# Soft MoE on linear attention: neighbouring loads joined into longer rows, their homes moved, and the last products and output chunks reordered

## The chip, the cores and the metric

The kernel runs on one core of one Trainium2 chip. The core has a matrix engine (PE, with a separate weight-load slot PEld), a vector engine (DVE), an activation engine (ACT), a general engine (POOL), and a queue engine (SP), which here only issues DMA transfers. 16 DMA engines move the bytes between HBM and the core's on-chip memory of 128 partitions. The metric is device time in microseconds, and less is better.

## What is computed

```python
kv = einsum('bhsd,bhse->bhde', k, v)            # 8 batches, 8 heads, 576 tokens, 64 wide
out = einsum('bhsd,bhde->bhse', q, kv)
x = out / sqrt(mean(out**2, -1) + 1e-6) * g_norm  # 4608 tokens x 512
logits = x @ phi                                # 32 slots: 8 experts x 4
d = exp(logits - logits.max(0));  d /= d.sum(0) + 1e-9
slot_input = d.T @ x
for e in range(8):                              # w1[e] 512 x 1024, w2[e] 1024 x 512
    slot_out[e] = relu(slot_input[e] @ w1[e]) @ w2[e]
c = exp(logits - logits.max(1));  c /= c.sum(1) + 1e-9
return c @ slot_out                             # 4608 x 512
```

All numbers are float32. Inputs are some 62 MB, half tokens and half expert weights, and the output is 9.4 MB.

## The kernel before

The host lays every input out so that each of the 128 partitions reads one contiguous piece. `kv` of a batch is 4608 floats (18 KB) per partition, and `q` of two batches together is as much. Each expert has one unit of `w1` and one of `w2`, of 4096 floats (16 KB) per partition. The `w2` units from 2 on are cut by output half: units 2, 3, 4 hold half 0 of experts 2 to 7, and units 5, 6, 7 hold half 1 of the same experts.

On chip one buffer, `arena`, of 160 KB per partition, holds all of it in turn. Tables give each piece its home, in KB: `KV_AT`, `Q_AT` and `W_AT` (line 36 on). `w1` of expert 7 has no home in the arena and goes into the buffer `xall` of the normalised tokens, once these are used up. The order of everything is written out by hand; no scheduler moves instructions.

The stages follow each other:

- Token phase. 36 tiles of 128 tokens (variable `T`, in order) go through products with the batch's `kv` matrix (`products`, line 236), squares, eviction, norm and logits. A batch's `kv` is made in three steps just ahead of the first tile that needs it: batch `b` starts at `first[b]`, and its `kv` tile is read at tiles `first[b]-3` and `first[b]-2`. Per group of 6 tiles an online softmax over tokens adds to the slot sums (`group_*`).
- Expert phase. `expert_h(e)` makes the hidden layer of expert e, `expert_y(e, hf)` adds its half `hf` of the output to `pY`. `combine(k)` makes the weights `c` for a third of the tokens.
- Output. `gather(hf)` copies a half of `pY`, `mix(hf)` makes the matrix `z`, and `output(hf, k, f)` makes one of six chunks of a half: four matmuls into two PSUM tiles `po`, one copy on ACT (line 655), one on DVE (line 657), and one transfer of 768 KB to HBM. PSUM tiles with tag `m` are three, shared by `po`, `ph` and `pz`.

All transfers are issued by SP, in program order. A load that must wait for its home (until PE has read the last of what lay there) holds back all loads behind it. The transfers then queue at the 16 DMA engines, in order of issue. Before the token phase SP issues 13 (lines 107 to 119); four groups more hang on tiles in `loads_behind` (line 122), and the rest of the weights are placed between the steps of the tail and of the expert phase.

`fill` puts matmuls on zeros where PE would idle.

Of the kernel before, what the change touches and what calls it, by code (L numbers as in the profile page):

```python
# [25 lines left out]
CT = 12  # L26
NCH = NT // CT
NX = 14
EARLY = (18, 2, 0)
LATE_FILL = (21, 5, 5, 2, 2)  # L30
TOK = 4608
UNIT = 4096
KB = 256
ARENA = 160 * KB
LATE = 6
KV_AT = (0, 36, 54, 90, 108, 0, 18, 36)
Q_AT = (18, 72, 142, 54)
W_AT = {
# [3 lines left out]
}  # L42
SCRATCH = 1024
EPS_RMS = 1e-6
EPS_SUM = 1e-9


@with_exitstack
def soft_moe_linear_attention(ctx: ExitStack, tc: tile.TileContext, kv_in, q_in, w1_in, w2_in, c_in, out):


    nc = tc.nc
# [11 lines left out]
    def place(at, n):  # L64
        return arena[:, at * KB : at * KB + n]

    def load_kv(b, g=None):
        lo, hi = (0, TOK) if g is None else (2304 * g, 2304 * g + 2304)
        nc.sync.dma_start(place(KV_AT[b], TOK)[:, lo:hi], kv_in[b, :, lo:hi])

    def load_q(g, half=None):
        lo, hi = {None: (0, TOK), 0: (0, 2048), 1: (2048, TOK)}[half]
        nc.sync.dma_start(place(Q_AT[g], TOK)[:, lo:hi], q_in[g, :, lo:hi])

    def kv_main(b, g):
        return place(KV_AT[b], TOK)[:, g * 2304 : g * 2304 + 2048]

    def kv_rest(b, g):
        return place(KV_AT[b], TOK)[:, g * 2304 + 2048 : g * 2304 + 2304]

    def q_main(b):
        return place(Q_AT[b // 2], TOK)[:, b % 2 * 2048 : b % 2 * 2048 + 2048].rearrange("p (r n) -> p r n", r=NPAIR)

    def q_rest(g):
        return place(Q_AT[g], TOK)[:, 4096:].rearrange("p (i r n) -> p i r n", i=2, r=NPAIR)


    def homes(kind, u):
        at = W_AT[kind, u]
        if at is None:  # L90
            return [xflat[:, :UNIT]]
        return [place(a, UNIT // len(at)) for a in at]

    def load_w(kind, u):
        parts = homes(kind, u)
        n = UNIT // len(parts)
        for i, t in enumerate(parts):
            nc.sync.dma_start(t, (w1_in if kind == "w1" else w2_in)[u, :, i * n : i * n + n])

    def w_block(kind, u, i):  # L100
        parts = homes(kind, u)
        n = UNIT // len(parts)
        k, at = divmod(i * 256, n)
        return parts[k][:, at : at + 256]


    load_kv(0, 0)
    nc.sync.dma_start(cst, c_in)
    load_kv(0, 1)
    load_q(0, 0)  # L110
    load_kv(1, 0)
    load_kv(1, 1)
    load_q(0, 1)
    load_kv(2)
    load_q(1, 0)
    load_kv(3)
    load_q(1, 1)
    load_kv(4)
    load_q(2)


    loads_behind = {
        9: lambda: (load_kv(5), load_kv(6), load_q(3), load_kv(7)),
        18: lambda: [load_w(k, e) for e in range(2) for k in ("w1", "w2")],
        27: lambda: [load_w("w1", e) for e in range(2, 5)],
        31: lambda: load_w("w1", 5),
    }

    nc.scalar.preload_act_table_set("natural_log_exp_and_others")
# [15 lines left out]
    for i in range(2):  # L145
        lo = 64 * i
# [20 lines left out]
    class Kv:  # L167
# [10 lines left out]
        def products(self, r):  # L178
            g, w = divmod(r, 2)
            main = kv_main(self.b, g).rearrange("p (r w c n) -> p r w c n", r=2, w=2, c=4)  # L180
            for c in range(4):
                for i in range(2):
                    lo = 64 * i
                    nc.tensor.matmul(  # L184
                        self.pkv[lo : lo + 64, w, g],
                        lhsT=main[:, w, 1, c, lo : lo + 64],
                        rhs=main[:, w, 0, c, lo : lo + 64],
                        start=c == 0 and (g == 0 or self.b == 0),
                        stop=False,
                    )  # L190
# [43 lines left out]
    sqs, mss, parts, r0s, rs_of = {}, {}, {}, {}, {}  # L234
# [201 lines left out]

    fill(EARLY[0])

    for g in range(2):
        kv = Kv(0, "o" if g else "kv", 2 if g else None)  # L440
        kv.products(2 * g)
        kv.products(2 * g + 1)
        kv.borders((g,))
        kv.slots((g,))
        fill(EARLY[1 + g])
    T_at, diag_at, pb_at, d_at, sums_at = {}, {}, {}, {}, {}
    for T in range(NT - 2):
        for b in range(1, B):
# [2 lines left out]
        o = products(T)  # L451
# [64 lines left out]
    group_max(G)  # L516
    for i in todo_sums:
        group_sum(*i)
    load_w("w1", 6)
    load_w("w1", 7)  # L520
    load_w("w2", 2)
    fill(LATE_FILL[0], home=ps.tile([P, 512], F32, tag="m", name="fill"), cols=512)
    group_max_T(G)
    group_max_row(G)
# [86 lines left out]
    def expert_y(e, hf):  # L611
        u, at = w2_unit(e, hf)
        for c in range(8):
            j = c % 4
            nc.tensor.matmul(  # L615
                pY[32 * j : 32 * j + 32, hf, :256],
                lhsT=hTs[e][:, c],
                rhs=w_block("w2", u, at + c),
                start=e == 0 and c < 4,
                stop=e == NE - 1 and c >= 4,  # L620
            )
# [16 lines left out]

    def output(hf, k, f):
        z = zs[hf]  # L640
        at = 6 * ((hf * NCH + k) * 2 + f)
# [16 lines left out]
        nc.sync.dma_start(out[hf, k, :, f], place(at, 4 * CT * NS))  # L658

    def halves(e):  # L660
        expert_y(e, 0)
        expert_y(e, 1)

    expert_h(0)
    load_w("w2", 3)
    expert_h(1)
    halves(0)
    load_w("w2", 4)
    load_w("w2", 5)
    combine(0)  # L670
    expert_h(2)
    halves(1)
    load_w("w2", 6)
    load_w("w2", 7)
    combine(1)
    for e in range(3, NE):
        expert_h(e)
# [3 lines left out]
        expert_y(e, 0)  # L681
    chunks = [(k, f) for k in range(NCH) for f in range(2)]
    gather(0)
    expert_y(2, 1)
    mix(0)
    expert_y(3, 1)
    output(0, *chunks[0])
    output(0, *chunks[1])
    expert_y(4, 1)
    expert_y(5, 1)  # L690
    output(0, *chunks[2])
    output(0, *chunks[3])
# [10 lines left out]
def build_program():  # L703
    import concourse.bacc as bacc

    nc = bacc.Bacc("TRN2", target_bir_lowering=False, num_devices=1, dynamic_dma_scratch_size=SCRATCH)
    shapes = {"kv": (B, P, TOK), "qt": (B // 2, P, TOK), "w1": (NE, P, UNIT), "w2": (NE, P, UNIT), "cs": (P, 129)}
# [48 lines left out]
```

## Time and profile before

| | |
|---|---|
| Runs | 176.03, 177.60, 177.36 us; median 177.36 |
| Profiled execution | 175.97 us, its span 174.2 us |
| Mean granted PE clock | 0.973 |
| Transfers issued by SP | 46: 16 for tokens, 17 for weights, 1 for constants, 12 for output |
| HBM | 61.93 MB read, 9.44 MB written |

The span runs from the first to the last instruction, and the profiled execution's own time has 1.8 us more around it. The transfers by kind, with the line's columns: what is written and read, how many, the size of one, and the median time from issue to landing:

```profile
arena<-in_w_dram SPq DMA_DIRECT2D x14, 2048.0 KB, 20.7
arena<-in_kv_dram SPq DMA_DIRECT2D x6, 2304.0 KB, 30.4
out_dram<-arena SPq DMA_DIRECT2D x12, 768.0 KB, 6.5
```

A time to landing counts everything that the transfer has to queue behind. Window rows give, for a stretch of the span, its length, each engine's busy time with its instructions, the granted PE clock, the busy share of the 16 DMA engines and what they moved. A share slightly above 1 comes from packets whose recorded times overlap a little.

### The profile page before, as it was taken

The page shows a single profiled execution, that of the slowest core. Times are in us where ns is not written, and L with a number is a line of the kernel's source. Part 1 is how long each engine was busy: PE and PEld are TensorE (multiplying, and loading weights), DVE is VectorE, ACT ScalarE, POOL GpSimd, SP SyncE. Part 2 cuts the span into 40 slices and gives each one's busy share as a digit, 9 for nine tenths or more (in the row PEclk, how much of TensorE's full clock was granted, in tenths as well). Part 3 has the DMA queues.
Part 4 walks back from the last instruction along what each step waited for, and adds up shares of the span by engine and source line. Part 5 has one row for each costly group of instructions (what it writes and reads, how often), then busy time and mean ns, then how long its engine had stood idle before and what let it go on. Part 6 is the DMA issues. An engine that isn't in the chain of part 4 may idle for free.

```text
span 174.2 us, 4772 instructions
## 1 busy us (share of the span) xinstructions
PE 148.2 (85%) x2024; PEld 108.9 (63%) x2024; DVE 88.3 (51%) x180; ACT 86.8 (50%) x224; POOL 55.7 (32%) x65
## 2 busy tenths in 40 slices
PE   7577799999989899999999769989999959989500
PEld 5456778889779788888996555456556424445200
DVE  1122156566486565466663778733888114457600
ACT  2036286986957957878779553102234003336400
POOL 6000067656546676266773568000000000000000
PEclk9999999999999999999999999999999999999955
DMA  5999999999999999999999999999999999999994
GB/s 188 416 429 426 439 414 432 420 432 440 414 432 423 421 431 420 420 427 436 429 418 419 433 418 433 429 429 406 440 421 419 425 425 426 386 398 406 419 419 199
DMA packets 6645, 71.68 MB, mean 411 GB/s; under 512 B 736, under 2 KB 864, under 8 KB 2400
## 3 DMA queue, kind: packets, MB, share of 16 engines
q1 hardware_dynamic: 6624, 71.37, 97.5%
q8 instruction: 16, 0.26, 0.6%
q14 instruction: 5, 0.04, 0.1%
HBM read 61.93 MB, written 9.44 MB: 410 GB/s over the span
## 4 chain that ended last, share of the span: by engine, by line
PE 46%; DMA 20%; ACT 11%; DVE 11%; issue 3%; POOL 2%; SPq 1%; POOLq 0%; DVEq 0%
PE o L252 17%; DMA arena<-in_w_dram 11%; DMA arena<-in_kv_dram 9%; PE kvp_kv L184 8%; PE po L647 5%; PE pY L615 4%; PE ph L597 3%; DVE logits L329 3%; PE pS L386 2%; DVE ms L275 2%; ACT arena L655 2%; POOL part L324 2%; ACT bd L219 2%; PE o L243 2%; ACT sq L262 2%
## 5 line engine op out<-in xcount | busy, mean ns | idle before, releaser
L252 PE MATMUL o<-bd,arena 128*128 128x192 f32 x256 | 49.4, 336 | 1.4 <-ACT xall L270 0.6
L252 PEld LDWEIGHTS o<-bd,arena 128*128 128x128 f32 x256 | 40.8, 190 | 4.7 <-ACT xall L270 1.6
L302 POOL TENSOR_TENSOR xall<-xall,r 128x512 f32<-128x512 f32 x34 | 34.8, 1044 | 0.0
L324 POOL TENSOR_TENSOR part<-part,r 128x512 f32<-128x512 f32 x17 | 17.8, 1049 | 51.5 <-DVE r L293 51.5
L329 DVE TENSOR_REDUCE logits<-part 128x64 f32<-128x512 f32 (+1 forms) x19 | 19.3, 1015 | 16.1 <-POOL part L324 16.0
L275 DVE TENSOR_REDUCE ms<-sq 128x16 f32<-128x1024 f32 (+1 forms) x19 | 22.0, 1156 | 6.2 <-ACT sq L262 6.2
L262 ACT ACTIVATE sq<-o 128x512 f32<-128x512 f32 x36 | 21.5, 596 | 6.5 <-PE o L252 5.9
L270 ACT COPY xall<-o 128x512 f32<-128x512 f32 x34 | 20.6, 607 | 0.0
L184 PE MATMUL kvp_kv<-arena 128*64 128x64 f32 x480 | 17.3, 225 | 3.6 <-DMA arena<-in_kv_dram 3.6
L655 ACT COPY arena<-po 128x768 f32<-128x768 f32 x12 | 9.3, 800 | 20.2 <-DMA arena<-in_w_dram 10.3
L184 PEld LDWEIGHTS kvp_kv<-arena 128*64 128x64 f32 x480 | 15.2, 138 | 6.5 <-DMA arena<-in_kv_dram 4.5
L615 PE MATMUL pY<-arena,xall 128*32 128x256 f32 x256 | 15.2, 380 | 2.4 <-DMA arena<-in_w_dram 2.4
L657 DVE COPY arena<-po 128x768 f32<-128x768 f32 x12 | 11.3, 956 | 8.0 <-PE po L647 7.2
L647 PE MATMUL po<-logits,z 32*128 32x384 f32 x96 | 13.7, 526 | 1.6 <-ACT arena L655 1.0
L615 PEld LDWEIGHTS pY<-arena,xall 128*32 128x32 f32 x256 | 8.0, 110 | 9.1 <-issue 3.2
L597 PE MATMUL ph<-arena,sTe 128*32 128x256 f32 x224 | 12.7, 379 | 0.3 <-DVE sTe L544 0.3
L269 ACT COPY part<-o 128x256 f32<-128x256 f32 x34 | 12.6, 371 | 0.0
L386 PE MATMUL pS<-xall,d 128*32 128x129 f32 x288 | 10.7, 276 | 2.1 <-ACT d L374 2.1
L283 ACT ACTIVATE r<-ms,eps 128x16 f32<-128x16 f32 x17 | 5.2, 308 | 12.8 <-DVE ms L275 12.6
L647 PEld LDWEIGHTS po<-logits,z 32*128 32x128 f32 x96 | 6.3, 183 | 8.2 <-ACT arena L655 4.1
L291 DVE SCALAR_TENSOR_TENSOR r<-ms,r 128x16 f32<-128x16 f32 x17 | 3.0, 175 | 15.3 <-ACT r L284 15.3
L597 PEld LDWEIGHTS ph<-arena,sTe 128*32 128x32 f32 x224 | 7.2, 110 | 5.2 <-DVE sTe L544 0.6
(88 smaller groups left out, 143.9 us busy)
## 6 DMA issues: line engine op xcount, KB each, us to landing
arena<-in_w_dram SPq DMA_DIRECT2D x14, 2048.0 KB, 20.7
arena<-in_kv_dram SPq DMA_DIRECT2D x6, 2304.0 KB, 30.4
out_dram<-arena SPq DMA_DIRECT2D x12, 768.0 KB, 6.5
arena<-in_kv_dram SPq DMA_DIRECT2D x4, 1152.0 KB, 10.1
arena<-in_qt_dram SPq DMA_DIRECT2D x2, 2304.0 KB, 32.1
arena<-in_qt_dram SPq DMA_DIRECT2D x2, 1280.0 KB, 23.2
arena<-in_qt_dram SPq DMA_DIRECT2D x2, 1024.0 KB, 16.4
xall<-in_w_dram SPq DMA_DIRECT2D x1, 2048.0 KB, 15.4
```

Source lines behind the costliest of these rows:

```text
L184: nc.tensor.matmul(self.pkv[lo : lo + 64, w, g], lhsT=main[:, w, 1, c, lo : lo + 64], rhs=main[:, w, 0, c, lo : lo + 64], start=c == 0 and ...
L252: nc.tensor.matmul(o[:, r, :192], lhsT=q_main(2 * g + i)[:, r, at : at + P], rhs=bds[i][:, r], start=True, stop=True)
L262: nc.scalar.activation(sqs[s][:, T - starts[s]], o[:, :, 32:160], AF.Square, scale=0.125)
L270: nc.scalar.copy(xts[T % NX][:, :, :128], o[:, :, 32:160])
L275: nc.vector.tensor_reduce(out=mss[s], in_=sqs.pop(s).rearrange("p t j (w d) -> p (t j w) d", w=2), axis=AX.X, op=ALU.add)
L302: nc.gpsimd.tensor_tensor(out=x, in0=x, in1=r[:, i].rearrange("p (j w) -> p j w", w=2).unsqueeze(3).to_broadcast([P, 4, 2, D]), op=ALU.mult,)
L324: engine.tensor_tensor(out=part, in0=part, in1=rs_of[s].unsqueeze(3).to_broadcast([P, STAGES[s], H, NS]), op=ALU.mult)
L329: nc.vector.tensor_reduce(out=L[:, pos(starts[s]) : pos(starts[s]) + STAGES[s]], in_=parts.pop(s).rearrange("p t h n -> p t n h"), axis=AX ...
L386: nc.tensor.matmul(pS[32 * j : 32 * j + 32], lhsT=ds[G][:, i], rhs=x[:, j], start=i == 0, stop=i == GROUPS[G] - 1)
L597: nc.tensor.matmul(ph[32 * j : 32 * j + 32], lhsT=sTe[:, (4 * e + c) * NS : (4 * e + c + 1) * NS], rhs=w_block("w1", e, 4 * c + j), start= ...
L615: nc.tensor.matmul(pY[32 * j : 32 * j + 32, hf, :256], lhsT=hTs[e][:, c], rhs=w_block("w2", u, at + c), start=e == 0 and c < 4, stop=e == ...
L647: nc.tensor.matmul(po[:, u, : CT * NS].rearrange("p (g x) -> p g x", g=2), lhsT=z[lo : lo + 32, f * P : (f + 1) * P], rhs=cT[k][lo : lo + 32],
```

## The change

Six transfers fewer, each larger, over the same bytes:

- `kv` 4 and `q` 2 become one tensor `t2` with rows of 36 KB; `kv` 6, `q` 3 and `kv` 7 become `t3` with rows of 54 KB; `kv` 5 stays alone. `kv` 0 to 3 and `q` 0 and 1 move to one tensor `head`, and are loaded in the same pieces and order as before.
- The weights lie in one flat tensor in the order of use. The first three loads each bring two units in rows of 32 KB: (w1 0, w2 0), (w1 1, w2 1), (w1 2, w1 3). All later units come singly.
- Homes are new, so that the parts of a joined row lie side by side: `kv` 3 goes where `kv` 0 was, `q` 2 behind `kv` 4, and `kv` 6, `q` 3, `kv` 7 over `q` 0, `kv` 1, `kv` 2.
- Loads hang on other tiles: the second pair on tile 21, the third on 26; one half of w2 2 comes ahead of w1 6. The three units of half 1 are all issued behind expert 1's products.
- The output buffers move up by 16 KB.
- At the end `mix(0)` and two chunks of half 0 come before the half 1 products of experts 2 and 3, one chunk more before experts 4 and 5, two more before 6 and 7; the last stands behind `gather(1)` instead of `mix(1)`.
- The first fills are half as many at twice the width.

```diff
-EARLY = (18, 2, 0)
+EARLY = (9, 1, 0)
...
-KV_AT = (0, 36, 54, 90, 108, 0, 18, 36)
-Q_AT = (18, 72, 142, 54)
+KV_AT = (0, 36, 54, 0, 90, 126, 18, 54)
+Q_AT = (18, 72, 108, 36)
...
+W_ROWS = (2, 2, 2, 1, 1, 1, 1, 1, 1, 1, 1, 1, 1)
...
+    def load_row(at, src):
+        nc.sync.dma_start(place(at, src.shape[-1]), src)
...
-    def load_w(kind, u):
-        parts = homes(kind, u)
-        n = UNIT // len(parts)
+    def load_w(*units, part=None):
+        lo = W_ORDER.index(units[0])
+        n = UNIT * len(units)
+        row = w_in[:, lo * UNIT * P : (lo * UNIT * P) + n * P].rearrange("o (p n) -> (o p) n", p=P)
+        parts = homes(*units[0])
+        if len(units) > 1:
+            parts = [place(W_AT[units[0]][0], n)]
...
     loads_behind = {
-        9: lambda: (load_kv(5), load_kv(6), load_q(3), load_kv(7)),
-        18: lambda: [load_w(k, e) for e in range(2) for k in ("w1", "w2")],
-        27: lambda: [load_w("w1", e) for e in range(2, 5)],
-        31: lambda: load_w("w1", 5),
+        9: lambda: load_row(KV_AT[6], t3_in),
+        18: lambda: load_w(("w1", 0), ("w2", 0)),
+        21: lambda: load_w(("w1", 1), ("w2", 1)),
+        26: lambda: load_w(("w1", 2), ("w1", 3)),
+        27: lambda: load_w(("w1", 4)),
+        31: lambda: (load_w(("w1", 5)), load_w(("w2", 2), part=1)),
     }
...
+    load_head(5, 0, TOK)
+    load_head(4, 2048, TOK)
+    load_row(KV_AT[4], t2_in)
+    load_row(KV_AT[5], kv5_in)
...
     halves(0)
-    load_w("w2", 4)
-    load_w("w2", 5)
+    load_w(("w2", 4))
     combine(0)
     expert_h(2)
     halves(1)
-    load_w("w2", 6)
-    load_w("w2", 7)
+    load_w(("w2", 5))
+    load_w(("w2", 6))
+    load_w(("w2", 7))
...
     gather(0)
-    expert_y(2, 1)
     mix(0)
-    expert_y(3, 1)
     output(0, *chunks[0])
     output(0, *chunks[1])
+    expert_y(2, 1)
+    expert_y(3, 1)
+    output(0, *chunks[2])
     expert_y(4, 1)
     expert_y(5, 1)
-    output(0, *chunks[2])
     output(0, *chunks[3])
+    output(0, *chunks[4])
     expert_y(6, 1)
     expert_y(7, 1)
     gather(1)
-    output(0, *chunks[4])
+    output(0, *chunks[5])
     mix(1)
-    output(0, *chunks[5])
```

The change moves instructions at two places. The first is SP's queue from `kv` 3 on, first before, then after (a row: line, operation, what is written and read, partitions x elements of a transfer, and in brackets the semaphores it waits for: DMAHW is another transfer's landing, PE the matrix engine).

```order
L69 DMA arena_64<-in_kv_dram 128x4608 [waits DMAHW1_49]
L73 DMA arena_64<-in_qt_dram 128x2560 [waits DMAHW2_49]
L69 DMA arena_64<-in_kv_dram 128x4608 [waits DMAHW3_49]
L73 DMA arena_64<-in_qt_dram 128x4608 [waits DMAHW4_49]
L69 DMA arena_64<-in_kv_dram 128x4608 [waits DMAHW5_49,PE_49]
L69 DMA arena_64<-in_kv_dram 128x4608 [waits DMAHW6_49,PE_49]
L73 DMA arena_64<-in_qt_dram 128x4608 [waits DMAHW7_49]
L69 DMA arena_64<-in_kv_dram 128x4608 [waits DMAHW0_49]
L98 DMA arena_64<-in_w1_dram 128x4096 [waits DMAHW2_49,DMAHW1_49,PE_49]
L98 DMA arena_64<-in_w2_dram 128x4096
L98 DMA arena_64<-in_w1_dram 128x4096 [waits DMAHW3_49]
L98 DMA arena_64<-in_w2_dram 128x4096 [waits DMAHW4_49]
```

```order
L71 DMA arena_64<-in_head_dram 128x4608 [waits DMAHW2_49,DMAHW1_49,PE_49]
L71 DMA arena_64<-in_head_dram 128x2560
L74 DMA arena_64<-in_t2_dram 128x9216 [waits DMAHW3_49]
L74 DMA arena_64<-in_kv5_dram 128x4608 [waits DMAHW4_49]
L74 DMA arena_64<-in_t3_dram 128x13824 [waits DMAHW6_49,DMAHW7_49,DMAHW5_49,PE_49]
L106 DMA arena_64<-in_w_dram 128x8192 [waits DMAHW2_49,DMAHW3_49,DMAHW0_49,PE_49]
L106 DMA arena_64<-in_w_dram 128x8192 [waits DMAHW4_49,PE_49]
```

Twelve transfers became seven; `kv` 3, the first row of each, now waits for PE too, and of the weights each pair waits for PE by itself.

The second place is PE's queue in the output stage, from the products that end half 0, before and after (pY collects the experts' products, pz is the mix, po an output chunk's PSUM tile: half, third, f, v).

```order
L615 MATMUL pY_1464<-arena_64,xall_65 32x256 x56
L635 MATMUL pz0_1753<-y0_1743,sel_93 128x256
L615 MATMUL pY_1464<-arena_64,xall_65 32x256 x8
L647 MATMUL po0_0_0_0_1765<-logits_104,z0_1755 128x384 x2
L647 MATMUL po0_0_0_1_1769<-logits_104,z0_1755 128x384 x2
L647 MATMUL po0_0_1_0_1774<-logits_104,z0_1755 128x384 x2
L647 MATMUL po0_0_1_1_1778<-logits_104,z0_1755 128x384 x2
L615 MATMUL pY_1464<-arena_64,xall_65 32x256 x16
```

```order
L625 MATMUL pY_1448<-arena_64,xall_65 32x256 x48
L645 MATMUL pz0_1729<-y0_1727,sel_89 128x256
L657 MATMUL po0_0_0_0_1733<-logits_100,z0_1731 128x384 x2
L657 MATMUL po0_0_0_1_1737<-logits_100,z0_1731 128x384 x2
L657 MATMUL po0_0_1_0_1742<-logits_100,z0_1731 128x384 x2
L657 MATMUL po0_0_1_1_1746<-logits_100,z0_1731 128x384 x2
L625 MATMUL pY_1448<-arena_64,xall_65 32x256 x16
```

Before, 8 products of expert 2 for half 1 stood ahead of the mix and 8 of expert 3 behind it; now all 16 stand behind the first two chunks.

More of the change, by code (lines that the diff above doesn't have):

```diff
@@ L35 @@
 LATE = 6
-KV_AT = (0, 36, 54, 90, 108, 0, 18, 36)
-Q_AT = (18, 72, 142, 54)
+KV_AT = (0, 36, 54, 0, 90, 126, 18, 54)
+Q_AT = (18, 72, 108, 36)
 W_AT = {
[3 rows of a table removed]
-}
[3 rows of a table added]
+}
+W_ROWS = (2, 2, 2, 1, 1, 1, 1, 1, 1, 1, 1, 1, 1)
+W_ORDER = [("w1", 0), ("w2", 0), ("w1", 1), ("w2", 1)] + [("w1", e) for e in range(2, NE)] + [("w2", u) for u in range(2, NE)]
 SCRATCH = 1024
@@ L48, in soft_moe_linear_attention @@
 @with_exitstack
-def soft_moe_linear_attention(ctx: ExitStack, tc: tile.TileContext, kv_in, q_in, w1_in, w2_in, c_in, out):
+def soft_moe_linear_attention(ctx: ExitStack, tc: tile.TileContext, head_in, t2_in, kv5_in, t3_in, w_in, c_in, out):
     nc = tc.nc
@@ L65, in place, with load_head @@
         return arena[:, at * KB : at * KB + n]
[L67 to L73, printed above, removed]
+    def load_head(u, lo, hi):
+        at = (KV_AT[0], KV_AT[1], Q_AT[0], KV_AT[2], Q_AT[1], KV_AT[3])[u]
+        nc.sync.dma_start(place(at, TOK)[:, lo:hi], head_in[u, :, lo:hi])
+    def load_row(at, src):
+        nc.sync.dma_start(place(at, src.shape[-1]), src)
     def kv_main(b, g):
@@ L92, in homes @@
         return [place(a, UNIT // len(at)) for a in at]
-    def load_w(kind, u):
-        parts = homes(kind, u)
-        n = UNIT // len(parts)
+    def load_w(*units, part=None):
[5 more added lines that the diff above has]
+            parts = [place(W_AT[units[0]][0], n)]
         for i, t in enumerate(parts):
-            nc.sync.dma_start(t, (w1_in if kind == "w1" else w2_in)[u, :, i * n : i * n + n])
+            if part not in (None, i):
+                continue
+            m = n // len(parts)
+            nc.sync.dma_start(t, row[:, i * m : i * m + m])
     def w_block(kind, u, i):
@@ L104, in w_block @@
         return parts[k][:, at : at + 256]
-    load_kv(0, 0)
+    load_head(0, 0, 2304)
     nc.sync.dma_start(cst, c_in)
[L109 to L119, printed above, removed]
-    loads_behind = {
-        9: lambda: (load_kv(5), load_kv(6), load_q(3), load_kv(7)),
-        18: lambda: [load_w(k, e) for e in range(2) for k in ("w1", "w2")],
-        27: lambda: [load_w("w1", e) for e in range(2, 5)],
-        31: lambda: load_w("w1", 5),
+    load_head(0, 2304, TOK)
+    load_head(2, 0, 2048)
+    load_head(1, 0, 2304)
+    load_head(1, 2304, TOK)
+    load_head(2, 2048, TOK)
+    load_head(3, 0, TOK)
+    load_head(4, 0, 2048)
+    loads_behind = {
+        9: lambda: load_row(KV_AT[6], t3_in),
[4 more added lines that the diff above has]
+        31: lambda: (load_w(("w1", 5)), load_w(("w2", 2), part=1)),
     }
@@ L435, in fill @@
             )
-    fill(EARLY[0])
+    fill(EARLY[0], cols=512)
     for g in range(2):
@@ L444, in soft_moe_linear_attention @@
         kv.slots((g,))
-        fill(EARLY[1 + g])
+        fill(EARLY[1 + g], cols=512)
+    load_head(5, 0, TOK)
+    load_head(4, 2048, TOK)
+    load_row(KV_AT[4], t2_in)
+    load_row(KV_AT[5], kv5_in)
     T_at, diag_at, pb_at, d_at, sums_at = {}, {}, {}, {}, {}
@@ L518, in soft_moe_linear_attention @@
         group_sum(*i)
-    load_w("w1", 6)
-    load_w("w1", 7)
-    load_w("w2", 2)
+    load_w(("w1", 6))
+    load_w(("w1", 7))
+    load_w(("w2", 2), part=0)
     fill(LATE_FILL[0], home=ps.tile([P, 512], F32, tag="m", name="fill"), cols=512)
@@ L640, in output @@
         z = zs[hf]
-        at = 6 * ((hf * NCH + k) * 2 + f)
+        at = 16 + 6 * ((hf * NCH + k) * 2 + f)
         st = place(at, 4 * CT * NS).rearrange("p (a n) -> p a n", a=4)
@@ L664, in soft_moe_linear_attention @@
     expert_h(0)
-    load_w("w2", 3)
+    load_w(("w2", 3))
     expert_h(1)
     halves(0)
-    load_w("w2", 4)
-    load_w("w2", 5)
+    load_w(("w2", 4))
     combine(0)
@@ L706, in build_program @@
     nc = bacc.Bacc("TRN2", target_bir_lowering=False, num_devices=1, dynamic_dma_scratch_size=SCRATCH)
-    shapes = {"kv": (B, P, TOK), "qt": (B // 2, P, TOK), "w1": (NE, P, UNIT), "w2": (NE, P, UNIT), "cs": (P, 129)}
+    shapes = {
+        "head": (6, P, TOK), "t2": (P, 2 * TOK), "kv5": (P, TOK), "t3": (P, 3 * TOK),
+        "w": (1, 2 * NE * P * UNIT), "cs": (P, 129),
+    }
     args = [nc.dram_tensor(f"in_{n}_dram", s, F32, kind="ExternalInput").ap() for n, s in shapes.items()]
@@ L743 @@
     cs = np.concatenate([ph, np.concatenate([g_norm, g_norm])[:, None]], axis=1)
-    arrays = {
-        "in_kv_dram": kv.reshape(B, P, TOK),
-        "in_qt_dram": qm,
-        "in_w1_dram": np.ascontiguousarray(w1),
-        "in_w2_dram": np.ascontiguousarray(w2),
+    kv = kv.reshape(B, P, TOK)
+    w = {("w1", e): w1[e] for e in range(NE)} | {("w2", u): w2[u] for u in range(NE)}
+    rows, u = [], 0
+    for n in W_ROWS:
+        rows.append(np.concatenate([w[k] for k in W_ORDER[u : u + n]], axis=1).reshape(-1))
+        u += n
+    arrays = {
+        "in_head_dram": np.stack([kv[0], kv[1], qm[0], kv[2], qm[1], kv[3]]),
+        "in_t2_dram": np.concatenate([kv[4], qm[2]], axis=1),
+        "in_kv5_dram": kv[5],
+        "in_t3_dram": np.concatenate([kv[6], qm[3], kv[7]], axis=1),
+        "in_w_dram": np.concatenate(rows)[None],
         "in_cs_dram": np.ascontiguousarray(cs),
```

6 rows, old and new, of the table W_AT are left out of this document.

## The prediction

> **What bounds the kernel.** I read the page's busy times first, then the slices of the span, then the DMA queues.
>
> ```profile
> span 174.2 us, 4772 instructions
> PE 148.2 (85%) x2024; PEld 108.9 (63%) x2024; DVE 88.3 (51%) x180; ACT 86.8 (50%) x224; POOL 55.7 (32%) x65
> DMA  5999999999999999999999999999999999999994
> GB/s 188 416 429 426 439 414 432 420 432 440 414 432 423 421 431 420 420 427 436 429 418 419 433 418 433 429 429 406 440 421 419 425 425 426 386 398 406 419 419 199
> DMA packets 6645, 71.68 MB, mean 411 GB/s; under 512 B 736, under 2 KB 864, under 8 KB 2400
> q1 hardware_dynamic: 6624, 71.37, 97.5%
> q8 instruction: 16, 0.26, 0.6%
> ```
>
> No compute engine is near the span, but the DMA digits are 9 from the second slice to the last but one, and SP's queue (q1) keeps 16 engines busy for 97.5% of it. The windows by stage (columns: stretch, five engines, PE clock, DMA share, GB/s) show where anything is left:
>
> ```profile
> 44.00:70.00 26.00, 25.02 (x376) 21.14 (x376) 15.94 (x32) 19.70 (x56) 15.99 (x16) 1.00 1.01 426
> 76.00:116.00 40.00, 36.41 (x486) 27.96 (x478) 25.40 (x58) 23.28 (x67) 19.58 (x20) 1.00 1.00 426
> 146.00:158.00 12.00, 11.24 (x118) 5.49 (x118) 5.90 (x9) 4.37 (x6) 0.00 (x0) 1.00 0.96 395
> 171.00:172.00 1.00, 0.00 (x0) 0.00 (x0) 0.00 (x0) 0.00 (x0) 0.00 (x0) 0.50 0.68 283
> 172.00:173.20 1.20, 0.00 (x0) 0.00 (x0) 0.00 (x0) 0.00 (x0) 0.00 (x0) 0.50 0.21 87
> ```
>
> From 4 to 171 us only the stretch 146 to 158 leaves room: 0.04 x 12 = 0.5 us per engine. The end is the same bound: the last output is issued at 164.74 and lands 8.5 us later, at 173.2, although an output can land in 5.3 (the one issued at 158.76), so it still queues behind others.
>
> ```profile
> 158.76 0.33 SPq L658 DMA_DIRECT2D out_dram<-arena  x1
> out_dram<-arena SPq DMA_DIRECT2D x1, 768.0 KB, 5.3
> 164.74 0.64 SPq L658 DMA_DIRECT2D out_dram<-arena  x1
> out_dram<-arena SPq DMA_DIRECT2D x1, 768.0 KB, 8.5
> ```
>
> So the time is the DMA queue's: bytes, a cost per row, and gaps. The change moves the same bytes. It can win by fewer rows, or by gaps, and lose by new gaps.
>
> **Longer rows.** What a row costs beside its bytes follows from two stretches with one row size each: 16 KB rows (96 to 116 us) and 6 KB rows (160 to 171 us).
>
> ```profile
> q1 hardware_dynamic: 585, 8.55, 100.5%
> q1 hardware_dynamic: 840, 4.61, 101.3%
> ```
>
> 8.55 MB are 522 rows of 16,384 B in 20 x 16 x 1.005 = 321.6 us, 616 ns each; 4.61 MB are 750 rows of 6,144 B in 11 x 16 x 1.013 = 178.3 us, 238 ns each. The difference, 378 ns for 10,240 B, is 0.0369 ns per byte, and 11 ns per row are left over (with each row's share of the small packet that ends a transfer). Check: an 18,432 B row would take 692 ns, or 426 GB/s, which is the row of 44 to 70 us. The first slices keep their pieces: the ten loads of "head" have the sizes of before. Joined are kv 4 with q 2 (36 KB rows), kv 6, q 3 and kv 7 (54 KB), and three weight pairs (32 KB): 6 transfers fewer of 46. With 8 rows on each of 16 engines: 6 x 8 x 11 ns = **0.5 us** less on every engine, all of it on the path. Bounds: no row shows one over 18 KB. If the hardware cut them up again the gain is 0. Above, byte time alone is 71.37 MB x 0.0369 / 16 = 165 us against 0.975 x 174.2 = 170 us busy, so all rows' overheads and the slow start together are 5 us, of which this removes 48 of 368 rows per engine (6645 packets less the 736 under 512 B, over 16). If long rows ran at the worst full stretch instead (395 GB/s for 146 to 158, which holds idle engines), 24.4 MB would take 61.8 instead of 57.3 us: a loss of 4.5. I take 0.5, since 16 and 18 KB lie on the line of the 6 KB rows.
>
> The Trainium skill, page "DMA: Bandwidth & Descriptors", section "Anatomy of one DMA", gives each DMA a fixed cost of about 2.0 us beside its bytes. By it six fewer would save 12 us, and the time would be about 164. The trace does not agree where transfers queue: the share is 1.00 in 76 to 116 us, with one transfer behind another. What the rows leave of it is rival 6.
>
> **The waits for homes.** SP issues in order, so one waiting load holds all behind it. It costs only if the engines run out. In SP's queue as the change's section shows it, kv 3 now waits for PE (it goes where kv 0 was), and the three loads of 18 KB that waited one by one are one load.
>
> ```profile
> L199 PE MATMUL kvp_o<-arena x8: 218/242/267, 10.4 to 10.5; 64*64 64x64 f32 x8
> 6.59 0.44 SPq L69 DMA_DIRECT2D arena<-in_kv_dram  x1
> arena<-in_kv_dram SPq DMA_DIRECT2D x1, 2304.0 KB, 28.6
> 34.86 0.33 SPq L69 DMA_DIRECT2D arena<-in_kv_dram  x1
> arena<-in_kv_dram SPq DMA_DIRECT2D x1, 2304.0 KB, 25.4
> 58.06 0.33 SPq L98 DMA_DIRECT2D arena<-in_w_dram  x1
> arena<-in_w_dram SPq DMA_DIRECT2D x1, 2048.0 KB, 18.1
> 80.93 0.33 SPq L98 DMA_DIRECT2D arena<-in_w_dram  x1
> arena<-in_w_dram SPq DMA_DIRECT2D x1, 2048.0 KB, 16.0
> 118.38 0.33 SPq L98 DMA_DIRECT2D arena<-in_w_dram  x1
> arena<-in_w_dram SPq DMA_DIRECT2D x1, 2048.0 KB, 13.2
> 15.55 0.33 SPq L73 DMA_DIRECT2D arena<-in_qt_dram  x1
> arena<-in_qt_dram SPq DMA_DIRECT2D x1, 2304.0 KB, 33.7
> 50.27 1.15 PE L184 MATMUL kvp_kv<-arena 128*64 128x64 f32 x32
> 72.98 1.15 PE L184 MATMUL kvp_kv<-arena 128*64 128x64 f32 x32
> ```
>
> Time to landing less the own bytes' time (5.5 us for 18 KB rows, 4.9 for 16 KB) is how long the engines had other work: the cover. Kv 3 stood at the end of a queue that lasted to 6.59 + 28.6 - 5.5 = 29.7, and PE is done with kv 0 at 10.5: 19 us of cover for the new wait. The 54 KB load waits for token tile 8, as kv 6 did at 34.86: 25.4 - 5.5 = 20 us. The first pair waits for tile 17, as w1 0 did at 58.06: 13 us. The second stands behind that pair (9.8 us of bytes). The third waits for tile 26, as w1 2 did at 80.93 with as many units ahead: 11 us. The tightest is w2 3, issued at 118.38 after the first hidden layer, as now: 13.2 - 4.9 = 8.3 us. So there is no gap: cost 0.
>
> A joined load lands as a whole. Kv 4 then lands with q 2, at 15.55 + 33.7 = 49.3 against its use at 50.27; kv 6 with kv 7, which was in when w1 0's own bytes began, at 58.06 + 13.2 = 71.3, against 72.98. PE keeps 1.0 and 1.7 us. If that went, PE would be late by as much, under the 8.3 us of cover: cost 0.
>
> **The end.** In PE's queue, shown with the change, the mix no longer stands behind 8 products that wait for the next weight.
>
> ```profile
> 141.48 1.07 PE L615 MATMUL pY<-arena,xall 128*32 128x256 f32 x16 [2.44 <-DMA arena<-in_w_dram]
> 146.15 0.35 SPq L658 DMA_DIRECT2D out_dram<-arena  x1
> 151.29 1.93 PE L615 MATMUL pY<-arena,xall 128*32 128x256 f32 x32
> ```
>
> That wait (2.44) and 1.07 of products leave its way, so the first output goes at about 143 instead of 146.15. It still queues behind the last weight, which PE meets at 151.29. This fills the 0.5 us of idle engines in 146 to 158, but at the end engines finish up to 2 us apart (171 to 173.2), so those that idle are likely the ones that ran ahead. The one that ends last is not helped, so I count 0 (bounds: 0 and -0.5). The sum: 175.97 of the profiled run (span 174.2 and 1.8 around it) - 0.5 = **175.5**. That run is the lowest of the four shown (176.03, 177.6, 177.36); from the median, 177.36, the same step gives 176.9. Between the two I say **176.2**.
>
> **The rivals.**
> 1. Long rows are cut up again and the change does nothing: 176.0 to 177.4, 176.7 in the middle. No row over 18 KB speaks either way.
> 2. Faster: the engines' unevenness shrinks. After 171 us 0.68 + 0.21 x 1.2 = 0.93 us of work per engine is left, and the last engine takes 2.2: it ends 1.3 us behind the mean. The 16 instruction packets, 0.006 x 16 x 174.2 / 16 = 1.05 us each, are one thing that can set one engine back. Were that gone: 176.2 - 1.3 = 174.9, and 174.2 from the profiled run. Against: nothing in the change aims at it.
> 3. Slower: half 1's outputs come late, since PE now does half 0 chunks ahead of the last pair of experts. The first half 1 output went at 158.76 and landed 5.3 us later. Its own 786 KB take 1.9 us at 409 GB/s; what a load costs beside its bytes and its queue is at most 2.7 us, from the first of all, which found the engines empty (5.5 to landing, 2.8 of it bytes):
>
> ```profile
> arena<-in_kv_dram SPq DMA_DIRECT2D x1, 1152.0 KB, 5.5
> ```
>
> So 0.7 to 3.4 us were queue; I take 2. Each us that PE is later than that is a us of the end. From 158.76 to 164.74 a chunk took 1.2 us; with all five chunks of half 0 in the way it is 6.0 late, 4.0 on the end: 180.2. With the two chunks that stand right ahead of the pair it is 2.4, nearly all of it hidden. Against: PE waits for that last weight anyway, and chunks done by then cost nothing.
> 4. Slower: instruction packets wait behind longer rows. Ten of them (7 + 3, rows below) fall in 44 to 102 us, where the rows grow from at most 0.69 us to at most 2.05 (54 KB at 0.0369). At 1.36 each, PE is up to 13.6 us late, 5.3 over the 8.3 of cover: 176.2 + 5.3 = 181.5. It decides only beyond 8.3 us; half of the bound hides.
>
> ```profile
> q8 instruction: 7, 0.11, 0.8%
> q14 instruction: 3, 0.02, 0.1%
> ```
>
> The Trainium skill, "DMA: Bandwidth & Descriptors", section "Queues, rings and completion order", speaks for it: a DMA engine takes turns between queues only at the end of a packet. By that rule the wait is as in 4; but PE is busy 25.0 of 26 us in 44 to 70, where such packets already wait behind 0.69 us rows, so it fetches ahead.
>
> 5. Slower: long rows run slower. At 409 GB/s (the lowest full stretch of the end, 158 to 172) the 24.4 MB cost 59.7 instead of 57.3 us: 176.7 + 2.4 = 179.1.
>
> ```profile
> 158.00:172.00 14.00, 5.08 (x38) 2.24 (x32) 5.30 (x6) 4.00 (x5) 0.00 (x0) 0.74 0.99 409
> ```
>
> 6. Faster: each transfer ends in a gap that a joined one loses. By the rows 2.5% of the span, 4.4 us, is all that is not busy, the start and the uneven end within it; over 46 transfers that is 0.1 each, 0.6 for six: 175.6. The share of 1.00 speaks against even that. (The skill's price for it is the 2.0 us above.)
>
> **How the numbers follow.** Forecast 0.56, rival 1 0.13, rival 2 0.16, rival 3 0.05, rival 4 0.03, rival 5 0.06, rival 6 0.01. What a measurement of this kernel can tell from no change is about 1%, 1.8 us. Forecast and rivals 1 and 6 lie within it; rival 2 is on the edge, and the spread of the runs (1.6 us) carries a little of the forecast over it: faster 0.16, within 1% 0.72, slower 0.12. The range, 174.4 to 178.0, takes in the forecast from both bases, rival 1 and most of rival 2, and leaves out the slow rivals.
>
> **What would show it.** Right: some 5,780 packets (6 x 144 fewer) and 71.7 MB; 428 GB/s or more in 44 to 100 us; DMA digits of 9 throughout; first output at about 143; an end some 0.5 us earlier at 8 us or more behind the last issue. Wrong: a slice of DMA under 9 inside the span, a last output that lands within 5.5 us of its issue (rivals 3 and 4), under 420 GB/s in 44 to 100 (rival 5), or an end over 1.3 us earlier with even engines (rival 2).

## The result, and the profile after

| | before | changed |
|---|---|---|
| median of 22 runs | 177.48 us | 175.81 us |
| lowest and highest | 175.85, 177.90 | 175.50, 176.46 |
| profiled execution (span) | 175.97 (174.2) | 175.68 (173.6) |

The ratio of the changed kernel's time to the old one's is 0.9936, with a 95% interval of 0.9915 to 0.9957: 0.6% less, or 1.1 us between the means. The medians lie further apart (1.7 us), because the old kernel's runs fall into two groups with nothing between them: 9 of these 22 lie around 176.05 (the lower group) and 13 around 177.60 (the upper). All 22 runs of the changed kernel lie in one group, at 175.84. Every execution of the old kernel that was profiled, the one of the prediction included, is of the lower group. One run of all those below, of the kernel with the last part of the new end, took 183.92 us at a mean granted clock of 0.843, where its other runs have 0.96 to 0.98, and is left out of every count.

So the gain has two parts. From the lower group to the changed kernel it is 176.05 - 175.84 = 0.2 us. The rest is the upper group's disappearance: 13/22 x (177.60 - 176.05) = 0.9 us.

The page of the changed kernel, as quoted of the old one:

```profile
span 173.6 us, 4743 instructions
PE 147.5 (85%) x2014; PEld 106.9 (62%) x2014; DVE 88.2 (51%) x180; ACT 86.8 (50%) x224; POOL 55.6 (32%) x65
DMA  5999999999899998999999999999999999999994
GB/s 178 420 434 425 448 404 445 404 498 425 387 429 476 477 433 352 419 432 427 423 449 410 412 415 417 429 430 419 434 423 421 419 434 416 409 425 410 421 421 169
DMA packets 5781, 71.67 MB, mean 413 GB/s; under 512 B 640, under 2 KB 768, under 8 KB 2304
q1 hardware_dynamic: 5760, 71.37, 97.4%
```

The packets fell from 6645 to 5781, which is 6 x 144: a row of 54 KB is one packet and was not cut up. The bytes are the same. The prediction named a slice under 9 as a sign of being wrong, and two digits are 8. They lie at 56 to 61 and 78 to 82 us, where rows of 54 and 32 KB run. But the first of these slices shows 477 GB/s, more than the byte cost of 0.0369 ns allows 16 engines (433), so a slice is too short to book long packets evenly. The longer windows show no gap (columns as before: stretch, engines, PE clock, DMA share, GB/s):

```profile
44.00:70.00 26.00, 25.03 (x374) 21.16 (x375) 16.08 (x33) 19.71 (x56) 15.98 (x16) 1.00 1.01 432
44.00:100.00 56.00, 54.00 (x771) 45.45 (x770) 34.04 (x70) 42.68 (x120) 31.81 (x32) 1.00 1.00 428
76.00:116.00 40.00, 36.40 (x494) 28.05 (x482) 25.54 (x57) 23.27 (x67) 19.70 (x20) 1.00 1.00 424
146.00:158.00 12.00, 10.60 (x120) 4.96 (x114) 5.54 (x7) 4.60 (x6) 0.00 (x0) 1.00 0.99 411
171.00:172.00 1.00, 0.00 (x0) 0.00 (x0) 0.00 (x0) 0.00 (x0) 0.00 (x0) 0.50 0.48 203
172.00:173.20 1.20, 0.00 (x0) 0.00 (x0) 0.00 (x0) 0.00 (x0) 0.00 (x0) 0.50 0.05 21
```

In 44 to 70 us, with 36 and 54 KB rows, the engines move 432 GB/s instead of 426; in 76 to 116 us, where 32 KB rows come first, 424 instead of 426. So the rate of a window is a rough reading. The packets' whole time is a better one: q1's share of the span was 97.5% of 174.2 us, which is 169.8 us per engine, and is 97.4% of 173.6 us, which is 169.1. The share in 146 to 158 rose from 0.96 to 0.99, because the first output is now issued at 143.15, three us earlier. Issue rows of the output, each with its time to landing:

```profile
143.15 0.34 SPq L668 DMA_DIRECT2D out_dram<-arena  x1
157.36 0.33 SPq L668 DMA_DIRECT2D out_dram<-arena  x1
out_dram<-arena SPq DMA_DIRECT2D x1, 768.0 KB, 6.1
163.76 0.97 SPq L668 DMA_DIRECT2D out_dram<-arena  x1
out_dram<-arena SPq DMA_DIRECT2D x1, 768.0 KB, 9.0
```

Half 1's first output (157.36) goes 1.4 us earlier than before and stands in more queue (6.1 us to landing instead of 5.3). The last one still has 9.0 us from issue to landing: the DMA queue is the bound up to the end, as it was.

### The profile page after: what moved, and what is told of

Same layout as the page of the kernel before. It is cut to its first block, busy times and chain, and to the rows that moved or that the text cites. A ratio compares the mean times of both kernels' runs of the same rounds, so it can differ in the third digit from the quotient of the medians.

```text
span 173.6 us, 4743 instructions
## 1 busy us (share of the span) xinstructions
PE 147.5 (85%) x2014; PEld 106.9 (62%) x2014; DVE 88.2 (51%) x180; ACT 86.8 (50%) x224; POOL 55.6 (32%) x65
## 2 busy tenths in 40 slices
DMA packets 5781, 71.67 MB, mean 413 GB/s; under 512 B 640, under 2 KB 768, under 8 KB 2304
## 3 DMA queue, kind: packets, MB, share of 16 engines
q1 hardware_dynamic: 5760, 71.37, 97.4%
## 4 chain that ended last, share of the span: by engine, by line
PE 47%; DMA 18%; DVE 12%; ACT 11%; issue 3%; POOL 2%; SPq 1%; POOLq 0%; DVEq 0%
PE o L258 17%; DMA arena<-in_w_dram 10%; DMA arena<-in_head_dram 9%; PE kvp_kv L190 8%; PE pY L625 5%; PE po L657 5%; PE ph L607 3%; DVE logits L335 3%; PE pS L392 2%; DVE ms L281 2%; DVE arena L667 2%; POOL part L330 2%; ACT bd L225 2%; PE o L249 2%; ACT sq L268 2%
## 5 line engine op out<-in xcount | busy, mean ns | idle before, releaser
L657 PEld LDWEIGHTS po<-logits,z 32*128 32x128 f32 x96 | 5.8, 183 | 9.4 <-ACT arena L665 5.0
```

The costliest lines, as they stand in the source:

```text
L657: nc.tensor.matmul(po[:, u, : CT * NS].rearrange("p (g x) -> p g x", g=2), lhsT=z[lo : lo + 32, f * P : (f + 1) * P], rhs=cT[k][lo : lo + 32],
```

## The experiments

Of each kernel 11 or 12 runs were compared with runs of the old kernel on the same chip; three more profiles of the old kernel are single runs. "Upper" counts runs above 176.6 us; between the old kernel's groups there was almost nothing (one run of 107 at 176.51). Over all these comparisons 65 of the 107 runs of the old kernel were upper.

### The rows alone

```diff
     def load_row(at, src):
-        nc.sync.dma_start(place(at, src.shape[-1]), src)
+        for lo in range(0, src.shape[-1], TOK):
+            nc.sync.dma_start(place(at, src.shape[-1])[:, lo : lo + TOK], src[:, lo : lo + TOK])
...
-            nc.sync.dma_start(t, row[:, i * m : i * m + m])
+            for o in range(0, m, UNIT):
+                z = min(o + UNIT, m)
+                nc.sync.dma_start(t[:, o:z], row[:, i * m + o : i * m + z])
```

> The changed kernel with every joined row loaded in the pieces of before (16 or 18 KB rows, 46 transfers, 6645 packets), same homes, order and end. Theory rows (48 rows fewer per engine at 11 ns each): 0.5 us longer than the changed kernel, 176.3 us, with 426 GB/s in 44 to 70 us instead of 432, and all runs at one level. Rival, joining also removes the upper level of the old runs (about 177.6 beside 176.0): two thirds of the runs near 177.5.

Measured: median 176.14, mean 176.16, and none of 12 runs upper. That is 0.32 us more than the changed kernel, and 0.46 us more than the changed kernel with the old fills (175.70, below), which was measured on the same chip.

```profile
span 174.5 us, 4751 instructions
q1 hardware_dynamic: 6624, 71.37, 97.3%
44.00:70.00 26.00, 25.02 (x373) 21.13 (x372) 16.24 (x33) 19.73 (x56) 15.95 (x17) 1.00 1.01 428
44.00:100.00 56.00, 54.18 (x772) 45.60 (x771) 34.15 (x70) 42.67 (x120) 31.75 (x33) 1.00 1.01 427
```

The packets' time is back at 169.8 us per engine (97.3% of 174.5). The rate was expected to fall to 426 GB/s in 44 to 70 us and fell to 428, and the kernel of the next experiment, which keeps the long rows, has 428 there too, so the rate settles nothing. By the times the rows are worth 0.3 to 0.5 us. The upper group stays away without them.

### The end alone, and the end taken back

The first kernel is the changed one with the old order of products and chunks at the end:

```diff
     gather(0)
+    expert_y(2, 1)
     mix(0)
+    expert_y(3, 1)
     output(0, *chunks[0])
     output(0, *chunks[1])
-    expert_y(2, 1)
-    expert_y(3, 1)
...
```

> The changed kernel with the products and output chunks of the end in the old order. Theory rows: the end order costs nothing on the engine that ends last, so 175.8 us and one level as in the changed kernel, with idle engines again in 146 to 158 (DMA share 0.96 instead of 0.99). Rival, the end order removed the upper level of the old runs: a part of the runs near 177.5.

Measured: 9 of 12 runs at 175.86 on average, as in the changed kernel, and 3 upper, at 177.41. So the rival came true in part. That 3 of 12 are fewer than the old kernel's 65 of 107 may be due to the rows, the homes or the fills; no run tells these apart. The second is the old kernel with the new end, and nothing else of the change.

> The kernel before with only the new end (mix and two chunks of half 0 ahead of half 1's products, and so on); rows, homes and loads as before. Theory, the end order removes the upper level (runs near 177.6): all twelve runs at the lower level of before, 176.0 (rows give nothing here), and a median ratio as large as that of the whole change less 0.3 us. Rival, homes or rows remove it: half or more of the runs near 177.5.

Measured: twelve of twelve at 176.04 on average, which is the old kernel's lower group, and none upper. In its profile the share of 146 to 158 us is 0.99 as in the changed kernel:

```profile
146.00:158.00 12.00, 10.32 (x116) 4.87 (x112) 5.54 (x7) 4.60 (x6) 0.00 (x0) 1.00 0.99 414
```

Two things follow. Filling the idle engines of that stretch is worth nothing by itself, since the time is that of the lower group. And the end order is what removes the upper group: it does so alone.

### The fills

The changed kernel with the old first fills (18 and 2 matmuls of 256 columns instead of 9 and 1 of 512).

```diff
-EARLY = (9, 1, 0)
+EARLY = (18, 2, 0)
...
-    fill(EARLY[0], cols=512)
+    fill(EARLY[0])
...
-        fill(EARLY[1 + g], cols=512)
+        fill(EARLY[1 + g])
```

> The changed kernel with the first fills as before (20 matmuls of 256 columns instead of 10 of 512, so 20 instructions more on PE). Theory rows: no difference, 175.8 us at one level. Rival, the fills' count shifts the instruction packets against the data and so removed the upper level: a part of the runs near 177.5, and the first instruction packet earlier (13.3 us instead of 16.3).

Measured: 175.70 on average, none of 12 upper. The fills don't matter to the groups; 0.1 us between this and the changed kernel is at the limit of what these runs tell.

### Looking for a profile of the upper group

The old kernel was run three times more, unchanged.

> The kernel before once more, for a profile that may fall on its upper level. If it does (about 177.6, span about 175.8), either the engine that ends last has one instruction packet more than in the profile shown (a step of about 1.6 us in the landings), or the engines idle somewhere for as long, or the start is later. At the lower level it repeats 176.0.

> The kernel before once more, for a profile on its upper level (3 in 5 of its runs). If it falls there (span about 175.8), the landings tell where 1.5 us come from: one more step of 1.6 us on the engine that ends last (an instruction packet), or idle engines between 146 and 160, or a later start.

> The same again; at least one of the two falls on the upper level with a chance of 5 in 6.

Measured: 176.14, 176.15 and 175.98, all of the lower group. The upper group never came before the profiler, so its cause had to be found from kernels that have it more, or less.

### Which part of the end

Three kernels, each the old one with one edit. The first moves only the mix and the first two chunks ahead, and so fills the place where PE waits 2.44 us for the weight of experts 2 and 3:

```diff
     gather(0)
-    expert_y(2, 1)
     mix(0)
-    expert_y(3, 1)
     output(0, *chunks[0])
     output(0, *chunks[1])
+    expert_y(2, 1)
+    expert_y(3, 1)
```

> The kernel before with the first part of the new end only: the mix and chunks 0 and 1 of half 0 ahead of the products of experts 2 and 3 for half 1; the rest of the end as before. Theory, the early first output (143 instead of 146 us) removes the upper level: twelve of twelve runs near 176.0. Rival, what comes behind it (half 1's outputs ready earlier) removes it: half or more of the runs near 177.5.

Measured: none of 11 upper, mean 176.05. The second moves only the last part.

```diff
     output(0, *chunks[3])
+    output(0, *chunks[4])
     expert_y(6, 1)
     expert_y(7, 1)
     gather(1)
-    output(0, *chunks[4])
-    mix(1)
     output(0, *chunks[5])
+    mix(1)
```

> The kernel before with the last part of the new end only: chunk 4 ahead of the products of experts 6 and 7, chunk 5 behind half 1's gather instead of behind its mix; the first output stays at 146. Theory, the early first output removes the upper level: here half or more of the runs stay near 177.5. Rival, half 1's outputs: twelve of twelve near 176.0.

Measured: 7 of 11 upper, but these at 176.91 on average, where the old kernel's upper runs on the same chip lie at 177.54. The third leaves the order alone and keeps PE busy in the wait.

```diff
     gather(0)
+    fill(6, home=ps.tile([P, 2, 512], F32, tag="m", name="fillG")[:, 0], cols=512)
     expert_y(2, 1)
```

> The kernel before with six matmuls on zeros where PE waits 2.4 us for a weight, ahead of the products of expert 2 for half 1. If the upper level comes from PE's clock falling in that gap, twelve of twelve runs near 176.0. If it comes from when the outputs reach the DMA queue, half or more stay near 177.5.

Measured: 1 of 11 upper, where the old kernel's share would give 6 or 7; the expectation, none, was missed by that one run. PE's timeline there, with the idle time and its releaser in brackets, and the first output:

```profile
139.65 1.47 PE L429 MATMUL fillG<-zeros 128*128 128x512 bf16 x6
141.48 1.07 PE L615 MATMUL pY<-arena,xall 128*32 128x256 f32 x16 [0.36 <-DMA arena<-in_w_dram]
146.15 0.35 SPq L658 DMA_DIRECT2D out_dram<-arena  x1
```

This kernel does nothing earlier than the old one: its products start at 141.48 and its first output goes at 146.15, to the hundredth as before. Only PE's wait is shorter, 0.36 instead of 2.44 us. So it is not the early output that removes the upper group, as the expectation of the first kernel had it, but that PE doesn't idle. That it is PE's clock which the idling changes is not shown by this run; the next one bears on it.

### PE idle for longer

The old kernel without the half 0 products of experts 2 to 7, which PE does just ahead of the wait. The loads are all there.

```diff
-    for e in range(NE - LATE, NE):
-        expert_y(e, 0)
```

> The kernel before without the half 0 products of experts 2 to 7 (so half 0 of the output holds experts 0 and 1 alone); all loads stay. PE then idles from about 134 to 141.5 us instead of 139 to 141.5, with the same transfers and the same order behind the gap. Theory, the upper level is PE's clock, halved behind an idle stretch, which makes half 1's outputs late: all runs at the upper level (177.5 or more), the profile's clock at 0.5 in a stretch behind 141.5, and the last output landing with little queue in front of it. Rival, the level has nothing to do with PE's clock: the mix of levels as before, or all near 176.0, since the DMA queue is the same.

Measured: 12 of 12 between 176.69 and 177.67, mean 177.27, though PE does less work. Only 5 of them reach the 177.5 that was expected of all. The profile, of a run at 177.64, shows why they are late. Windows (the third number from the end is PE's granted clock), then PE's timeline:

```profile
133.90:137.20 3.30, 0.00 (x0) 0.00 (x0) 1.67 (x5) 0.47 (x1) 0.00 (x0) 1.00 1.00 427
137.20:141.60 4.40, 0.00 (x0) 0.00 (x0) 0.00 (x0) 0.00 (x0) 0.00 (x0) 0.51 1.02 436
141.60:147.50 5.90, 5.85 (x42) 2.37 (x44) 0.42 (x1) 0.00 (x0) 0.00 (x0) 0.50 0.97 411
147.50:152.00 4.50, 4.24 (x56) 1.90 (x50) 1.92 (x2) 1.50 (x2) 0.00 (x0) 1.00 0.74 303
152.00:156.00 4.00, 3.75 (x48) 1.56 (x40) 1.92 (x2) 1.50 (x2) 0.00 (x0) 1.00 0.88 359
...
141.65 1.94 PE L615 MATMUL pY<-arena,xall 128*32 128x256 f32 x16 [7.80 <-DMA arena<-in_w_dram]
143.52 1.22 PE L635 MATMUL pz<-y,sel 128*128 128x256 f32 x2
144.67 1.93 PE L615 MATMUL pY<-arena,xall 128*32 128x256 f32 x16
```

PE stops at 133.9. Its clock is halved 3.3 us later and stays so until 147.5, 5.9 us after PE has work again. The products of one expert take 1.94 us instead of 1.07. In those 5.9 us PE does 2.9 us of work, and it is 2.9 us late from there on: nothing up to the last output (issued at 167.62 instead of 164.74) gives any of it back, because every wait for a weight is over when PE gets there. The DMA share of 0.74 and 0.88 shows the queue running dry. Issue rows of the first output of each half:

```profile
149.03 0.35 SPq L658 DMA_DIRECT2D out_dram<-arena  x1
out_dram<-arena SPq DMA_DIRECT2D x1, 768.0 KB, 4.0
161.64 0.33 SPq L658 DMA_DIRECT2D out_dram<-arena  x1
out_dram<-arena SPq DMA_DIRECT2D x1, 768.0 KB, 4.1
```

They go at 149.03 instead of 146.15 and at 161.64 instead of 158.76, and now land in 4.0 and 4.1 us, close to the shortest of this run's outputs (3.5), so with little queue in front of them. The last output was expected to land so too, but takes 7.3 us, against 8.5 before. The span grew by 175.9 - 174.2 = 1.7 us. Of 2.9 us of lateness, 1.2 were hidden by the queue.

### The wait's length and the upper group

The kernels in the order of the idle time that ends at the weight of experts 2 and 3 in their profiled executions (none: PE's next products come behind two output chunks):

```
idle us   kernel            upper runs
none      changed           0 of 22
none      new end           0 of 12
none      mix first         0 of 11
none      pieces, old fills,
          output in pairs   0 of 36
0.36      gap filled        1 of 11
1.08      old end, rows     3 of 12
1.60      tail first        7 of 11
2.44      before            65 of 107
7.80      long gap          12 of 12 (lowest 176.69)
```

The order is coarser than its numbers look. The old kernel's four profiles show 2.44, 1.71, 2.54 and 2.08 us for the same wait, and tail first has the same instructions ahead of it, so its 1.60 us is one more value of that wait and not a step of its own.

The mean granted clocks of the runs are in keeping with PE's clock as the cause, but prove little. Of the old kernel's 42 lower runs 33 had a mean clock of 0.979 or more, and none of the 65 upper ones had more than 0.973. A mean clock of 0.980, typical of the lower group, is 2 x 0.020 x 174.3 = 7.0 us at half clock; 0.972 to 0.965, typical of the upper, is 2 x 0.028 x 175.8 = 9.8 to 2 x 0.035 x 175.8 = 12.3 us. Read so, an upper run has 3 to 5 us more of it. But a mean doesn't say where, and a low one doesn't make an upper run: 12 of the 22 runs of the changed kernel have 0.973 or less and lie in one group. The lower run that the prediction was read from has 0.973 too, with all of its half clock from 164.7 us on, when PE has done its last matmul. Nor does a mean hold all of it: in the old kernel's second profile (mean 0.980) the first 32 products for `kv` take 1.98 us instead of 1.15, in a window whose clock is given as 1.00.

What a short wait does to the clock can be read at the start of two profiles, where the old kernel and the kernel with the new end are the same code. PE waits there for the first piece of `kv`. Its row, the one of the next 32 products of this kind, and the window of 8 to 11 us, first in the old kernel's profile, then in the other:

```profile
6.25 1.15 PE L184 MATMUL kvp_kv<-arena 128*64 128x64 f32 x32 [1.48 <-DMA arena<-in_kv_dram]
9.31 1.15 PE L184 MATMUL kvp_o<-arena 128*64 128x64 f32 x32 [0.37 <-DMA arena<-in_kv_dram]
8.00:11.00 3.00, 2.22 (x45) 1.78 (x45) 0.44 (x2) 0.67 (x4) 0.00 (x0) 1.00 1.00 423
```

```profile
6.33 1.15 PE L184 MATMUL kvp_kv<-arena 128*64 128x64 f32 x32 [1.46 <-DMA arena<-in_kv_dram]
9.47 1.98 PE L184 MATMUL kvp_o<-arena 128*64 128x64 f32 x32
8.00:11.00 3.00, 2.77 (x33) 2.33 (x35) 0.45 (x2) 0.61 (x3) 0.00 (x0) 0.50 1.01 427
```

In the second the clock is halved from 8.0 to 11.4 us, after a wait of 1.46 us and with PE at work again, and 32 products take 1.98 instead of 1.15 us. In the first a wait of 1.48 us changes nothing. So waits of this length go with a halved clock in one execution and not in another. At the start this costs no time (that run took 175.93 us).

The Trainium skill, page "TensorE: Matmul & The Clock Gate", section "What's actually happening", says that the clock is gated by PE's activity in windows of some 3.4 us, which run freely and are not aligned to the kernel. The 3.3 us from PE's stop to the halved clock in the kernel with the long wait, and the 3.4 us of half clock at the start above, agree with it, and windows that lie differently in each execution would explain why the same wait lowers the clock in some runs and not in others. The page gives a whole idle window as the condition; the fall above came 1.7 us after a wait of 1.46 us had ended, with PE at work in between, so a shorter wait seems to do.

### Output in pairs

The row cost suggested one more step: the changed kernel with each third's two chunks in one transfer.

```diff
-        nc.sync.dma_start(out[hf, k, :, f], place(at, 4 * CT * NS))
+        if f == 1:
+            nc.sync.dma_start(out[hf, k].rearrange("p f n -> p (f n)"), place(at - 6, 8 * CT * NS))
```

> The changed kernel with each two output chunks of one third sent as one transfer (6 of 1536 KB with 12 KB rows instead of 12 of 768 KB with 6 KB rows). Theory, a row costs about 10 ns beside its bytes on every engine up to the end: 48 rows fewer once more, 0.3 to 0.5 us less than the changed kernel, 175.4 us, at one level. Rival, the second chunk of each pair holds the first back, so that the engines run dry between pairs: no gain or a loss up to 1.2 us (one chunk's time on PE), 175.8 to 177.0, with a DMA share under 0.95 in 146 to 160.

Measured: median 175.70, mean 175.80, from 175.26 to 176.54: no difference from the changed kernel that these runs can tell, and a wider spread. The first output now goes at 145.75, behind its partner, and the queue has gaps in the output stage:

```profile
span 174.7 us, 4732 instructions
q1 hardware_dynamic: 4896, 71.37, 96.6%
145.75 0.35 SPq L669 DMA_DIRECT2D out_dram<-arena  x1
146.00:158.00 12.00, 10.60 (x124) 4.66 (x116) 5.40 (x7) 3.97 (x6) 0.00 (x0) 1.00 0.92 386
```

The share is 0.92 where it was 0.99. This profile is of the slowest of the 12 runs (176.54). Its packets take 96.6% of 174.7 us, which is 168.8 us per engine where the changed kernel has 169.1. So the 48 rows fewer do save some 0.3 us of packet time, and the idle engines use it up.

## Why the prediction was right, and where it was wrong

The time, the range and "within 1%" came out: 175.81 against 176.2 and 174.4 to 178.0, and 0.6% less. But only a part of it for the reasons given, and that 176.2 lies so near is partly luck: it was set between two bases, and the same step from the median gave 176.9, 1.1 us too long, because the upper group's disappearance was not foreseen.

**The bound.** Right for the profile that it was read from. The DMA queue carries the time up to the end in the lower group and in the changed kernel.

**Longer rows, 0.5 us.** The mechanism was right, and the size about right: taking them back costs 0.32 to 0.46 us, or 7 to 10 ns for each of 48 rows per engine instead of 11, and puts 0.7 us on the packets' time (169.1 to 169.8; the shares are rounded, so 0.5 to 0.9). (The 368 rows per engine of the working are q1's; the 6645 packets named there would give 369. Nothing hangs on it.) Rival 1 (rows cut up again) falls with the packet count, rival 5 (slower long rows) with 428 GB/s in 44 to 100 us and the shorter packets' time. Rival 6 was not tested apart; six more transfers with all their gaps cost 0.3 to 0.5 us in all, so the 12 us by the fixed cost that the prediction cites are not there. The Trainium skill, page "DMA: Bandwidth & Descriptors", section "Anatomy of one DMA", gives that cost for transfers issued by the general engine, and here SP issues them.

**The waits for homes, 0.** Right: with the homes, the places of the loads and the fills alone between them (the run in pieces, 176.16, against the new end on the old kernel, 176.04) nothing is gained, the 0.1 us more is at the limit of what these runs tell, and the windows show no gap. That PE keeps up behind the joined landings is seen in its rows of 44 to 100 us, where it is busy 54.0 of 56 as before (53.9). With that rival 4, instruction packets behind long rows, falls too.

**The end, 0.** This is the step that failed: a term put at 0 that was worth 0.9 us on average. It was right on the idle engines: filling them gives nothing in the lower group. But it saw in PE's wait of 2.44 us only a delay of the first output, hidden by the queue. That the wait itself makes the upper group is shown: six matmuls on zeros in it leave 1 upper run of 11. That it does so through the clock is inferred, from the kernel with the long wait. By this reading PE came late to half 1's outputs in three of five runs of the old kernel, and the new end removes the wait, which gains more than the rows.

**The spread of the runs.** The text put the forecast between the profiled run and the median and carried the 1.6 us along as a spread. Four numbers (175.97, 176.03, 177.36, 177.60) already showed two groups, and a profile of one of them can't speak for the other. The step from the profile, 175.5, was for the lower group, and the changed kernel's 175.84 is the number to hold against it.

**Rival 3.** Its mechanism is real in the kernel with the long wait. In the changed kernel half 1's outputs come 1.4 us earlier than before; by the reading above it is the old one in which they come late. Its cover was taken as 2 us, and the kernel with the long wait showed 1.2. Rival 2, less unevenness, is not what happened: the last engine was as far behind as before. After 171 us, 0.48 + 0.05 x 1.2 = 0.54 us per engine are left, and the last output lands 1.8 us in (163.76 + 9.0), 1.2 us behind that mean where it was 1.3.

What stays open: the halved clock behind this wait was seen in the profile of the kernel with the long wait, not in an upper run of the old kernel, of which there is no profile. That it is the same there is inferred from the filled wait and from the order by idle time. The sizes don't close: with the 1.2 us of cover of the long wait's profile, the 1.5 us between the groups need some 2.7 us of lateness, or 5.5 us at half clock (an estimate), and the half clock seen after a short wait lasted 3.4. All seven profiles of kernels with both groups are of lower runs, which by their shares has a chance of about 1 in 170, so a profiled execution may not be like the others. And why tail first has its upper runs 0.6 us lower was not tried; its first output of half 1 goes at 158.32 instead of 158.76, which would explain a part.

## What to carry to other kernels

When a kernel's runs fall into groups, find out which of them the profile shows before working from it, and count what the other would cost. A wait of PE that the DMA queue hides may not be free: if the clock falls in it or behind it, what follows runs at half speed, so try work or fills in waits of a us or more ahead of a tail that PE feeds. Here, where transfers of 16 KB rows already queued without gaps, longer rows gave some 10 ns for each row saved.

## What the runs showed of the hardware

- With a wait of 7.80 us PE's clock fell to half 3.3 us after its last work and came back 5.9 us after new work had begun, although PE was busy for all of that.
- After a wait of 1.46 us the clock was halved for 3.4 us in one profile; after 1.48 us at the same place it was not in another. In two profiles of the old kernel it fell 1.1 us (163.7 to 164.7) and 3.4 us (163.9 to 167.3) after PE's last matmul.
- A wait of 1.71 to 2.54 us in four profiled executions went with two groups of times, 1.54 us apart, in 61% and 39% of 107 runs; with the wait filled to 0.36 us, 1 of 11 runs was in the upper group.
- Rows of 54 KB ran as one packet each. In 44 to 100 us, with rows of up to 54 KB, the engines moved 428 GB/s; with rows of 16 and 18 KB there, 426 and 427.
